# Attention's tables computed on the chip in place of five loads, and the second chunk's q loaded and scored earlier

## The chip, the cores and the metric

The kernel runs on one core of a Trainium2 chip. The metric is the device time of one execution in microseconds (us). Before the change it is 579.93 us, the median of three runs (579.83 to 580.10).

## What is computed

A decaying linear attention is followed by two feed-forward layers. Cut to what matters (q, k and v are 2 x 8 x 768 x 64, the layers have 1536 tokens of 512 features):

```python
gamma = 1.0 - 2.0 ** (-5.0 - np.arange(H))
for t in range(S):
    state = gamma * state + outer(k[:, :, t], v[:, :, t])
    y[:, :, t] = (q[:, :, t] @ state) / np.sqrt(D)
x = y.transpose(0, 2, 1, 3).reshape(B * S, H * D)
xn = x / np.sqrt(np.mean(x * x, -1) + 1e-6) * rms_g
x = (silu(xn @ w_gate) * (xn @ w_val)) @ w_out
h = x @ w_in
out = np.maximum(0.01 * h, h) @ moe2_w_out
```

## The kernel before

**Attention by chunks.** The 1536 tokens are cut into 12 chunks of 128, six for each batch entry. A chunk needs two loads of 512 KB: `qkT` (q and k by feature, called q0 to q11 in the list of loads) and `kv` (k and v by token, k0 to k11). On TensorE a chunk c is scored (`sc`, line 187), its keys, scaled by their decay (`kd`, lines 160 and 168), are multiplied with v to the state's increment (`ou`, line 213), the running state is applied to the decayed q (`yi`, line 238) and the masked scores to v (`he`, line 254). VectorE multiplies the scores with the mask (`ds`, line 199), makes the decayed keys of six chunks (`kd`, line 160; ScalarE makes those of four, line 168), updates the state (`up`, lines 228 and 230) and adds up squares (`fa`, `sa`, lines 281 and 286). GpSimd multiplies q by its decay (`qs`, line 176). ScalarE squares the output and applies the gains (`sq`, `xg`, lines 266 and 274). `qs` of a chunk c has to stand ahead of its `yi`, `ds` ahead of `he`, `kd` ahead of `ou`, and `ou` ahead of `up`.

**Tables.** The mask (128 x 2 x 4 x 128 float32), the decay of q (`qdec_sb`), of the keys (`kdecs`), of the state (`sdecs`), the gains `rms_g` and an identity come from the host. `kdecs` and `sdecs` are loaded for the first of their places only; the others are powers of it: a matmul (`across`, line 1186) spreads the state's decays over the partitions, a reciprocal (line 1195) makes `turn` of them, and four multiplications (line 1197) and three (line 1206) fill the tables.

**What sets the order.** All loads but one stand in SyncE's queue in the order of the string `LOADS` (line 39): q and k as above, m the mask (two transfers), g the gains, s and d the decays of state and q, i the identity, w a weight tile (line 396). `kdecs` is loaded from ScalarE's queue (line 1177). The instructions of every engine up to the middle of the first layer's first group are written out by hand in `ORDER` (lines 48 to 62), one token for a step: `sc0` scores chunk 0, `wm1` runs four matmuls on zeros into the bank that the scores of chunk 1 will take, `tb`, `ts` and `tk` make the tables, `load` queues the loads of q11 and k11, g0:P to g0:L convert a weight tile. Each engine keeps the order of the tokens. Before the first token, seven matmuls on zeros (`keep_warm`, line 189) run on TensorE.

**After attention.** The steps behind `ORDER` are placed by a planner that gives costs to conversions and evacuations; TensorE then runs weight products without a break to the end.

Of the kernel before, what the change touches and what calls it, by code (L numbers as in the profile page):

```python
# [8 lines left out]
F32 = mybir.dt.float32  # L9
# [4 lines left out]
AF = mybir.ActivationFunctionType  # L14
ALU = mybir.AluOpType
AX = mybir.AxisListType

P = 128
CH = 128
# [16 lines left out]
SEVEN1 = (1, 2)  # L36
RAWS = 3
WARM = 7
LOADS = "q0 k0 m g s k1 q1 d q2 q3 k2 k3 q4 k4 q5 w w q6 w q7 k6 k8 k7 k5 i q8 q9 k9 q10 k10"
EARLY = 5  # L40
FIXED = 14
PLAIN = ("g0", "g1", "v0", "v1")
# [3 lines left out]

KD = (0, 1, 2, 3, 6, 7)
ORDER = """
sc0 kd0 ou0 ds0 tb ts wm1 tk he0 load kd1 up0 sc1 sq0 qs1 xg0 ou1 ds1 qs2 sc2 up1 fa0 yi1 qs3 ds2 he1 kd2 sa0 ou2 kd3
sq1 sc3 xg1 fa1 up2 qs4 yi2 ds3 kd4 ou3 sa1 sc4 up3 qs5 sc5 ds4 g0:P yi3 ds5 ou4 g1:P g0:1 he2 up4 g0:2 he3 g1:1 sq2  # L50
g0:3 to0 xg2 fa2 g1:2 sc6 me0 sa2 sq3 g0:4 sc7 xg3 ds6 rs0 v0:P yi4 kd6 ds7 ou6 qs7 kd8 he4 up6 yi5 kd7 v0:1 sq4 fa3
ou7 g0:H fa4 he5 sa3 xg4 g0:L up7 sq5 v0:2 sc8 sa4 xg5 fa5 v0:3 sc9 qs9 ds8 yi7 kd9 ds9 qs8 ou8 sp0 v0:4 to1 up8 qs10
# [13 lines left out]
def chain_kernel(ctx: ExitStack, tc: tile.TileContext, qk_t, kv, w1, w2, mask, qdec, kdec, sdec, rms_g, ident, out):  # L66
    nc = tc.nc
    NCHUNK = kv.shape[0]
    NPAIR = 4
    D = 64  # L70
# [3 lines left out]
    CPB = NCHUNK // 2  # L74
# [16 lines left out]
    const = attn_pools.enter_context(tc.tile_pool(name="const", bufs=1))  # L91
# [4 lines left out]
    mask_sb = const.tile([P, 2, NPAIR, CH], F32, name="mask_sb")  # L96
    qdec_sb = const.tile([P, NPAIR, CH], F32, name="qdec_sb")
    kdecs = const.tile([P, CPB - 1, 2 * NPAIR, 1], F32, name="kdecs")
    sdecs = const.tile([P, CPB - 2, NPAIR, 1], F32, name="sdecs")
    turn = const.tile([P, 2, NPAIR], F32, name="turn")  # L100
    g_sb = const.tile([P, NPAIR, 1], F32, name="g_sb")
    ident_sb = const.tile([P, P], F32, name="ident_sb")
    ones = const.tile([P, 1], F32, name="ones")
    expo = const.tile([P, 2], F32, name="expo")
    one_of = const.tile([P, 2], F32, name="one_of")
    ready = const.tile([P, 2], F32, name="ready")
    state = [const.tile([P, NPAIR, D], F32, name=f"state{i}") for i in range(4)]

# [3 lines left out]
    def acc_bank(i, name):  # L112
        return ps_acc.tile([P, 512], F32, tag=f"acc{i}", name=name)
# [7 lines left out]

    ch = {}
    xh, xl, xg = {}, {}, {}
    tables = {"d": (qdec_sb, qdec), "s": (sdecs[:, 0], sdec), "g": (g_sb, rms_g), "i": (ident_sb, ident)}

    def load(*items):
        for what in items:
            n, c = what[0], int(what[1:] or 0)
            if n == "w":
                fetch()  # L130
            elif n == "m":
                for j in range(2):
                    nc.sync.dma_start(out=mask_sb[:, j], in_=mask[:, j])
            elif n in tables:
                nc.sync.dma_start(out=tables[n][0], in_=tables[n][1])
            else:
                if c not in ch and EARLY <= c < EARLY + len(SPARE):
                    t = xp.tile([P, 4, 512], F32, tag=SPARE[c - EARLY], name=f"qkv{c}")
                    ch[c] = {"qkT": t[:, :2], "kv": t[:, 2:]}
                elif c not in ch:  # L140
                    ch[c] = {m: units.tile([P, 2, 512], F32, tag="u", name=f"{m}{c}") for m in ("qkT", "kv")}
                if n == "q":
                    nc.sync.dma_start(out=ch[c]["qkT"], in_=qk_t[c])
                else:
                    nc.sync.dma_start(out=ch[c]["kv"], in_=kv[c])

    nrm = {}

    def block_of(c):
        return max(i for i in range(NB) if offs[i] <= c * CH)  # L150
# [38 lines left out]
    def keep_warm(c, n=WARM):  # L189
        s = ch.setdefault(c, {})  # L190
        s["sc"] = ps_sc.tile([P, 2, NPAIR, CH], F32, tag="sc", name=f"sc{c}")
        for _ in range(n):
            nc.tensor.matmul(out=s["sc"][:, 0], lhsT=warm[:, :P], rhs=warm, start=True, stop=True)
# [197 lines left out]
    def fetch():  # L391
        if fetched[0] < min(len(sources), taken[0] + RAWS):
            key, src = sources[fetched[0]]
            fetched[0] += 1
            raw[key] = raws.tile([P, 512, 2], I32, tag="raw", name=f"raw_{key}")
            nc.sync.dma_start(out=raw[key].rearrange("p n two -> p (n two)"), in_=src.bitcast(I32))
# [108 lines left out]
    def queue(unit):  # L505
        key, after, ops = unit
        cost = COST_SUM if dict(wq)[key] is None else COST
        take = lambda names: [(key, *cost[n], ops.pop(n)) for n in names if n in ops]
        if key in index and dict(wq)[key] is None:
            converting.extend(tails + take("123H4h"))  # L510
            tails[:] = take("Ll")
            return
        converting.extend(take("P12"))
        if after is not None and ("P" in opened_units[after][2] if after in opened_units else True):
            converting.append((after, *COST["P"], lambda: prepare(after)))
        converting.extend(tails + take("34H"))
        tails[:] = take("L")
# [410 lines left out]
    def in_pairs(ops):  # L928
        both = [[ops[n] for n in (f"{i}", f"h{i}") if n in ops] for i in range(4)]
        return [lambda b=b: [do() for do in b] for b in both if b] + [ops[f"l{i}"] for i in range(4) if f"l{i}" in ops]  # L930
# [236 lines left out]
    steps = plan()  # L1167

    warm = const.tile([P, 512], mybir.dt.bfloat16, name="warm")
    nc.vector.memset(warm, 0.0)  # L1170
    nc.vector.memset(ones, 1.0)
    nc.vector.memset(expo, -0.5)
    nc.vector.memset(one_of, 0.0)
    for j in range(2):
        nc.vector.memset(one_of[j * D:j * D + 1, j:j + 1], 1.0)
    nc.scalar.activation(out=ready, in_=expo, func=AF.Silu)
    nc.scalar.dma_start(out=kdecs[:, 0], in_=kdec)
    load(*LOADS.split())

    def pair(p):  # L1180
        return 2 * p, 2 * p + 1

    def across():
        nrm["bank"] = acc_bank(3, "norm")
        for j in range(2):
            nc.tensor.matmul(
                out=nrm["bank"][:, j * NPAIR:(j + 1) * NPAIR],
                lhsT=one_of[:, j:j + 1].to_broadcast([P, P]),
                rhs=sdecs[:, 0, :, 0],
                start=True,  # L1190
                stop=True,
            )

    def tables_k():
        nc.vector.reciprocal(out=turn, in_=nrm["bank"][:, :2 * NPAIR].rearrange("p (j a) -> p j a", j=2))
        for i in range(1, CPB - 1):
            nc.vector.tensor_tensor(
                out=kdecs[:, i, :, 0].rearrange("p (a j) -> p j a", j=2),
                in0=kdecs[:, i - 1, :, 0].rearrange("p (a j) -> p j a", j=2),
                in1=turn,  # L1200
                op=ALU.mult,
            )

    def tables_s():
        for i in range(1, CPB - 2):
            nc.vector.tensor_tensor(out=sdecs[:, i], in0=sdecs[:, i - 1], in1=sdecs[:, 0], op=ALU.mult)

    terms = {}

# [11 lines left out]
    def layers():  # L1221
# [6 lines left out]
    }  # L1228
    by_pair_of = {"to": total, "me": mean, "rs": rsqrt, "sp": spread, "xs": scaled, "hi": high, "lo": rest}
    alone = {  # L1230
        "open": reopen, "layers": layers, "load": lambda: load("q11", "k11"), "tk": tables_k, "ts": tables_s,
        "tb": across,
    }
    by_step = {"M": product_high, "N": product_low, "C": consume}

    def do(token):
        if token in alone:
            alone[token]()
        elif ":" in token:
            convert_step(*token.split(":"))  # L1240
        elif token[:2] in by_chunk:
            by_chunk[token[:2]](int(token[2:]))
        elif token[:2] in by_pair_of:
            by_pair_of[token[:2]](pair(int(token[2:])))
        elif token[0] == "T":
            terms.pop(token[1:])()
        else:
            n, f, b = token[1], int(token[2]), int(token[3])
            if token[0] in by_step:
                by_step[token[0]](n, f, b)  # L1250
            elif token[0] == "D":
                down(0, f, b)
            else:
                (upper if token[0] == "U" else lower)((n, f, b))

    with tc.manual_schedule():
        keep_warm(0)
        for token in ORDER.split():
            do(token)
        for unit in opened_units.values():  # L1260
            if unit[2]:
                queue(unit)
        sums.extend(in_pairs(terms))
# [98 lines left out]
```

## Time and profile before

| | before |
|---|---|
| median of three runs | 579.93 us |
| time of the profiled execution | 579.99 us |
| its span in the trace | 578.2 us |
| TensorE (PE) busy | 567.9 us (98%) |
| VectorE (DVE) busy | 498.5 us (86%) |
| ScalarE (ACT) busy | 404.6 us (70%) |
| GpSimd (POOL) busy | 39.3 us (7%), 48 instructions |
| share of 16 DMA engines of SyncE's and ScalarE's transfers | 27.2% |

The span is the time from the first to the last instruction of the program; 1.79 us of the execution's own time lie around it. PEld is the weight load of TensorE, SPq, POOLq and so on the sequencers that issue and wait. All times of rows are counted from the span's start. A row of instructions ends, in brackets, with the idle time of the engine before it and what ended it. A row with "x7" merges seven instructions, and its time is that from the first's start to the last's end; matmuls are pipelined, so a busy TensorE need not be one at its peak.

### The profile page before, as it was taken

Reading aid. Unit: us, or ns where it says so; the run is one execution under the profiler, and the core shown is the slowest. Engines: PE = TensorE matmul, PEld = TensorE weight load, DVE = VectorE, ACT = ScalarE, POOL = GpSimd, SP = SyncE. Lnnn points to the kernel's source line nnn. Section 1 sums busy time; section 2 is a strip of 40 time slices with the busy share of each in tenths; the row PEclk is TensorE's granted clock in tenths of the full one; section 3 lists DMA queues with packets and bytes.
Section 4 is the critical chain, followed back from the end, with each engine's and each line's share of the span. In section 5 each row is a group of like instructions: output and inputs, shape, how many; then the busy total and the mean of one; then the engine's idle time right before and its main releaser. Section 6 shows DMA issues by size and latency. Waiting matters only on the chain.

```text
span 578.2 us, 8479 instructions
## 1 busy us (share of the span) xinstructions
PE 567.9 (98%) x3086; PEld 466.8 (81%) x3086; DVE 498.5 (86%) x920; ACT 404.6 (70%) x738; POOL 39.3 (7%) x48
## 2 busy tenths in 40 slices
PE   8899999999999999999999999999999999999997
PEld 5788788888888888888888878878888888888886
DVE  5799989986676899977899999999999989995793
ACT  2789767986666557877647589989867985676330
POOL 2332100010000000001000100000100020002100
PEclk9999999999999999999999999999999999999999
DMA  8991332442101221326220222224412253101545
GB/s 333 409 394 56 110 109 74 140 149 77 54 26 68 74 74 37 109 73 146 73 74 0 74 73 74 73 74 135 157 54 88 78 121 99 37 1 23 124 85 135
DMA packets 34922, 60.13 MB, mean 104 GB/s; under 512 B 19392, under 2 KB 19776, under 8 KB 34880
## 3 DMA queue, kind: packets, MB, share of 16 engines
q1 hardware_dynamic: 31728, 52.24, 27.2%
q0 software_dynamic: 3008, 7.34, 5.6%
q8 instruction: 24, 0.39, 0.3%
q14 instruction: 18, 0.15, 0.1%
q10 hardware_dynamic: 144, 0.00, 0.0%
HBM read 51.19 MB, written 8.39 MB: 103 GB/s over the span
## 4 chain that ended last, share of the span: by engine, by line
PE 87%; DMA 6%; DVE 4%; ACT 2%; issue 1%; SPq 0%; POOL 0%; DVEq 0%; POOLq 0%; ACTq 0%
PE X L795 11%; PE ao L625 9%; PE Z L795 8%; PE iX L995 8%; PE i L594 8%; PE ap L625 7%; PE v L594 7%; PE g L594 6%; PE vX L995 5%; PE gX L995 5%; PE iZ L995 4%; PE vZ L995 2%; PE gZ L995 2%; DMA qkv<-in_qk_t 2%; PE iY L995 2%; DMA qkv<-in_kv 2%
## 5 line engine op out<-in xcount | busy, mean ns | idle before, releaser
L625 PE MATMUL ap<-w_p,gp_0h 128*128 128x512 f32 (+1 forms) x130 | 39.7, 386 | 0.0
L594 PE MATMUL i<-x2h,w_i 128*128 128x512 f32 x128 | 32.3, 389 | 0.0
L594 PE MATMUL g<-xh,w_g 128*128 128x512 f32 x128 | 31.8, 390 | 0.0
L594 PE MATMUL v<-xh,w_v 128*128 128x512 f32 x128 | 31.7, 390 | 0.0
L625 PE MATMUL ao<-go_0h,w_o 128*128 128x512 f32 x96 | 31.0, 389 | 0.0
L625 PEld LDWEIGHTS ap<-w_p,gp_0h 128*128 128x128 f32 x130 | 24.3, 188 | 5.0
L594 PEld LDWEIGHTS g<-xh,w_g 128*128 128x128 f32 x128 | 23.9, 188 | 5.2 <-issue 0.2
L594 PEld LDWEIGHTS i<-x2h,w_i 128*128 128x128 f32 x128 | 24.0, 188 | 5.0
L594 PEld LDWEIGHTS v<-xh,w_v 128*128 128x128 f32 x128 | 23.9, 188 | 5.0
L625 PE MATMUL ap<-w_p,gp_0l 128*128 128x512 f32 (+1 forms) x65 | 25.1, 386 | 0.0
L933 ACT ACTIVATE more<-i 128x512 f32<-128x512 f32 x16 | 9.6, 599 | 22.1 <-PE i L594 22.0
L995 PE MATMUL iX<-th,w_si 128*128 128x512 f32 x64 | 20.7, 397 | 1.2 <-ACT iu L1012 0.7
L625 PEld LDWEIGHTS ao<-go_0h,w_o 128*128 128x128 f32 x96 | 18.0, 188 | 3.7
L995 PE MATMUL iZ<-x2h,w_si 128*128 128x512 f32 x64 | 20.2, 391 | 0.0
L497 DVE TENSOR_TENSOR w_o<-wa_o,w_o 128x512 fp32r<-128x512 f32 x12 | 8.2, 686 | 12.1 <-ACT w_o L493 12.1
L625 PE MATMUL ao<-go_0l,w_o 128*128 128x512 f32 x48 | 18.7, 389 | 0.0
L594 PE MATMUL g<-xl,w_g 128*128 128x512 f32 x64 | 17.2, 391 | 0.0
L594 PE MATMUL v<-xl,w_v 128*128 128x512 f32 x64 | 17.2, 391 | 0.0
L199 DVE TENSOR_TENSOR a<-sc,mask_sb 128x1024 f32<-128x1024 f32 (+1 forms) x13 | 14.5, 1135 | 3.1 <-PE sc L187 3.0
L826 DVE TENSOR_TENSOR y2acc<-X,y2acc 128x512 f32<-128x512 f32 x26 | 17.0, 681 | 0.2 <-PE X L795 0.2
L594 PE MATMUL i<-x2l,w_i 128*128 128x512 f32 x64 | 17.1, 389 | 0.0
L995 PEld LDWEIGHTS iX<-th,w_si 128*128 128x128 f32 x64 | 11.8, 188 | 5.2 <-ACT iu L1012 1.4
(364 smaller groups left out, 1814.5 us busy)
## 6 DMA issues: line engine op xcount, KB each, us to landing
raw_i<-in_w SPq DMA_DIRECT2D x16, 512.0 KB, 3.6
raw_p<-in_w SPq DMA_DIRECT2D x16, 512.0 KB, 3.6
raw_g<-in_w SPq DMA_DIRECT2D x12, 512.0 KB, 3.6
raw_v<-in_w SPq DMA_DIRECT2D x12, 512.0 KB, 3.4
raw_o<-in_w SPq DMA_DIRECT2D x12, 512.0 KB, 3.5
qkT<-in_qk_t SPq DMA_DIRECT2D x7, 512.0 KB, 6.6
kv<-in_kv SPq DMA_DIRECT2D x7, 512.0 KB, 8.1
out<-more POOLq DMA_DIRECT2D x12, 256.0 KB, 5.1
```

What stands on the lines that cost most here:

```text
L199: nc.vector.tensor_tensor(out=s["a"][:, j], in0=s["sc"][:, j], in1=mask_sb[:, j], op=ALU.mult)
L497: v.tensor_tensor(out=u[:, 1, :], in0=a, in1=u[:, 0, :].bitcast(F32), op=ALU.subtract)
L594: nc.tensor.matmul(out=dst, lhsT=lhs, rhs=rhs, start=(n == 0), stop=(n == len(pairs) - 1), skip_group_check=True)
L625: nc.tensor.matmul(out=acc["b"][m][:, c:c + cut], lhsT=lhs, rhs=rhs[:, c:c + cut], start=(start and n == 0), stop=(stop and n == 2), skip_ ...
L795: nc.tensor.matmul(out=acc[side][m], lhsT=lhs, rhs=rhs, start=(start and f == fs[0] and k == 0), stop=(f == fs[-2] and k == 2), skip_group ...
L826: nc.vector.tensor_tensor(out=dst, in0=banks[m], in1=dst, op=ALU.add)
L933: nc.scalar.activation(out=a, in_=x, func=AF.Prelu, alpha=0.01)
L995: nc.tensor.matmul(out=dst, lhsT=lhs, rhs=rhs, start=(start and n == 0), stop=(n == 5), skip_group_check=True)
```

## The change

The loads of the mask, of both decays (q and state) and of the identity are gone. The gains move to ScalarE's queue. GpSimd makes a ramp (`iota`, column minus partition) in the place of the identity and sets 56 single columns to constants. VectorE compares the ramp with zero (`tri`), fills the mask's tile with the powers of every head's decay by seven doublings, and scales it row by row with the decay of the keys and `tri`; ScalarE copies the powers into `qdec_sb` in between. This stands ahead of the first token. `kdecs` beyond its second place and `sdecs` are made later (`tk`), the identity by a comparison of the ramp (`id`). In the list of loads q1 and k1 come second, and in the order of the work `wm1` follows `sc0`, `sc1` and `qs1` come ahead of `he0`, `sc2` comes behind `yi1`.

```diff
-LOADS = "q0 k0 m g s k1 q1 d q2 q3 k2 k3 q4 k4 q5 w w q6 w q7 k6 k8 k7 k5 i q8 q9 k9 q10 k10"
+LOADS = "q0 k0 q1 k1 q2 q3 k2 k3 q4 k4 q5 w w q6 w q7 k6 k8 k7 k5 q8 q9 k9 q10 k10"
...
 ORDER = """
-sc0 kd0 ou0 ds0 tb ts wm1 tk he0 load kd1 up0 sc1 sq0 qs1 xg0 ou1 ds1 qs2 sc2 up1 fa0 yi1 qs3 ds2 he1 kd2 sa0 ou2 kd3
+sc0 wm1 kd0 ou0 ds0 sc1 qs1 he0 load kd1 up0 sq0 xg0 ou1 ds1 qs2 up1 fa0 yi1 sc2 qs3 ds2 tk id he1 kd2 sa0 ou2 kd3
 sq1 sc3 xg1 fa1 up2 qs4 yi2 ds3 kd4 ou3 sa1 sc4 up3 qs5 sc5 ds4 g0:P yi3 ds5 ou4 g1:P g0:1 he2 up4 g0:2 he3 g1:1 sq2
...
-    turn = const.tile([P, 2, NPAIR], F32, name="turn")
+    turn = const.tile([P, 2 * NPAIR], F32, name="turn")
...
-    one_of = const.tile([P, 2], F32, name="one_of")
+    steps_of = const.tile([P, 4, 2 * NPAIR, 1], F32, name="steps_of")
...
-            elif n == "m":
-                for j in range(2):
-                    nc.sync.dma_start(out=mask_sb[:, j], in_=mask[:, j])
-            elif n in tables:
-                nc.sync.dma_start(out=tables[n][0], in_=tables[n][1])
...
-    nrm = {}
+    nrm = {"bank": acc_bank(3, "norm")}
+    heads_of = [(j, a, 1.0 - 2.0 ** (-5.0 - 2 * a - j)) for j in range(2) for a in range(NPAIR)]
+    powers = mask_sb.rearrange("p j a t -> p (j a) t")
+    tri = state[3].rearrange("p a d -> p (a d)")[:, :CH]
+
+    def constants():
+        nc.gpsimd.iota(
+            ident_sb, pattern=[[1, CH]], base=0, channel_multiplier=-1, allow_small_or_imprecise_dtypes=True
+        )
+        for i, (j, a, g) in enumerate(heads_of):
+            nc.gpsimd.memset(powers[:, i, 0:1], g / D ** 0.5)
+        for k in range(4):
+            for i, (j, a, g) in enumerate(heads_of):
+                nc.gpsimd.memset(steps_of[:, k, i], g ** (8 << k))
+        for j, a, g in heads_of:
+            nc.gpsimd.memset(turn[:, 2 * a + j:2 * a + j + 1], g ** -CH)
+        for j, a, g in heads_of:
+            nc.gpsimd.memset(sdecs[j * D:(j + 1) * D, 0, a], g ** CH)
+
+    def decays():
+        nc.vector.tensor_scalar(tri, ident_sb, 0.0, None, ALU.is_ge)
+        for k in range(7):
+            n = 1 << k
+            out = powers[:, :, n:2 * n]
+            if k < 3:
+                nc.vector.scalar_tensor_tensor(
+                    out=out,
+                    in0=powers[:, :, :n],
+                    scalar=D ** 0.5,
+                    in1=powers[:, :, n - 1:n].to_broadcast([P, 2 * NPAIR, n]),
+                    op0=ALU.mult,
+                    op1=ALU.mult,
+                )
+            else:
+                nc.vector.tensor_tensor(
+                    out=out,
+                    in0=powers[:, :, :n],
+                    in1=steps_of[:, k - 3].to_broadcast([P, 2 * NPAIR, n]),
+                    op=ALU.mult,
+                )
+        for j in range(2):
+            own = slice(j * D, (j + 1) * D)
+            nc.scalar.activation(out=qdec_sb[own], in_=mask_sb[own, j], func=AF.Copy)
+        tables_k(1, 2)
+        for j, a, _ in heads_of:
+            nc.vector.scalar_tensor_tensor(
+                out=mask_sb[:, j, a],
+                in0=mask_sb[:, j, a],
+                scalar=kdecs[:, 1, 2 * a + j],
+                in1=tri,
+                op0=ALU.mult,
+                op1=ALU.mult,
+            )
+
+    def identity():
+        nc.vector.tensor_scalar(ident_sb, ident_sb, 0.0, None, ALU.is_equal)
...
     warm = const.tile([P, 512], mybir.dt.bfloat16, name="warm")
+    constants()
     nc.vector.memset(warm, 0.0)
     nc.vector.memset(ones, 1.0)
     nc.vector.memset(expo, -0.5)
-    nc.vector.memset(one_of, 0.0)
-    for j in range(2):
-        nc.vector.memset(one_of[j * D:j * D + 1, j:j + 1], 1.0)
-    nc.scalar.activation(out=ready, in_=expo, func=AF.Silu)
-    nc.scalar.dma_start(out=kdecs[:, 0], in_=kdec)
-    load(*LOADS.split())
...
-    def across():
-        nrm["bank"] = acc_bank(3, "norm")
-        for j in range(2):
-            nc.tensor.matmul(
-                out=nrm["bank"][:, j * NPAIR:(j + 1) * NPAIR],
-                lhsT=one_of[:, j:j + 1].to_broadcast([P, P]),
-                rhs=sdecs[:, 0, :, 0],
...
-    def tables_k():
-        nc.vector.reciprocal(out=turn, in_=nrm["bank"][:, :2 * NPAIR].rearrange("p (j a) -> p j a", j=2))
-        for i in range(1, CPB - 1):
...
-    def tables_s():
-        for i in range(1, CPB - 2):
-            nc.vector.tensor_tensor(out=sdecs[:, i], in0=sdecs[:, i - 1], in1=sdecs[:, 0], op=ALU.mult)
+    def tables_k(first=2, end=CPB - 1):
+        for i in range(first, end):
+            nc.vector.tensor_tensor(
+                out=kdecs[:, i, :, 0], in0=kdecs[:, i - 1, :, 0], in1=turn, op=ALU.mult
+            )
+            if i > 1:
+                nc.vector.tensor_tensor(out=sdecs[:, i - 1], in0=sdecs[:, i - 2], in1=sdecs[:, 0], op=ALU.mult)
...
+    nc.scalar.dma_start(out=kdecs[:, 0], in_=kdec)
+    nc.scalar.dma_start(out=g_sb, in_=rms_g)
+    nc.scalar.activation(out=ready, in_=expo, func=AF.Silu)
+    load(*LOADS.split())
+
     with tc.manual_schedule():
         keep_warm(0)
+        decays()
         for token in ORDER.split():
             do(token)
```

## Rows read from the trace of the kernel before

**Rows 1.** The page's chain that ended last, its shares of the span by engine.
```profile
PE 87%; DMA 6%; DVE 4%; ACT 2%; issue 1%; SPq 0%; POOL 0%; DVEq 0%; POOLq 0%; ACTq 0%
```

**Rows 2.** The chain of waits, first 110 us: start, time and what, in us.
```profile
2.12 4.96 DMA mask_sb<-in_mask
...
27.29 9.14 DMA qkv<-in_kv
...
69.38 3.87 PE g L594 x16
```

**Rows 3.** Stretches: busy us of PE, PEld, DVE, ACT, POOL; granted clock, DMA share, GB/s.
```profile
0.00:10.00 10.00, 7.91 (x63) 4.46 (x63) 4.42 (x19) 1.49 (x2) 0.20 (x4) 1.00 0.80 299
10.00:20.00 10.00, 9.50 (x162) 8.11 (x160) 7.74 (x14) 3.54 (x12) 5.19 (x4) 1.00 1.03 408
...
69.00:569.00 500.00, 498.71 (x2197) 410.20 (x2194) 437.70 (x800) 357.41 (x615) 19.92 (x28) 1.00 0.28 81
```

**Rows 4.** The loads that go, first 60 us: KB each, us from issue to landing.
```profile
mask_sb<-in_mask SPq DMA_DIRECT2D x2, 256.0 KB, 4.8
qdec_sb<-in_qdec SPq DMA_DIRECT2D x1, 256.0 KB, 5.4
ident_sb<-in_ident SPq DMA_DIRECT2D x1, 64.0 KB, 9.1
kdecs<-in_kdec ACTq DMA_DIRECT2D x1, 4.0 KB, 3.9
```

**Rows 5.** GpSimd's instructions in order of time, first 50 us: start, us.
```profile
0.24 0.10 POOL L1355 MEMSET const-float32-0.0<- 128x1 f32 x1 [0.24 <-issue]
...
0.34 0.10 POOL L1355 MEMSET const-uint8-127<- 128x1 uint8 x1
10.56 3.92 POOL L176 TENSOR_TENSOR qs<-qkT,qdec_sb 128x512 f32<-128x512 f32 x3 [10.11 <-DMA qdec_sb<-in_qdec]
```

**Rows 6.** Line 176 in the first 15 us: what GpSimd's sequencer does for it.
```profile
L176 POOLq MODIFY_POOL_CONFIG  x2: 8/10/11, 0.7 to 0.8; - x2
```

**Rows 7.** VectorE, with a load and an instruction of ScalarE, in order of time.
```profile
0.74 0.40 ACTq L1177 DMA_DIRECT2D kdecs<-in_kdec  x1
...
5.80 0.69 DVE L160 TENSOR_TENSOR kd<-kv,kdecs 128x512 f32<-128x512 f32 x1 [4.40 <-DMA kv<-in_kv]
...
8.45 0.78 DVE L1197 TENSOR_TENSOR kdecs<-kdecs,turn 128x8 f32<-128x8 f32 x4
...
10.12 0.60 ACT L266 ACTIVATE sq<-y 128x512 f32<-128x512 f32 x1 [7.45 <-PE y L254]
...
14.41 0.68 DVE L160 TENSOR_TENSOR kd<-kv,kdecs 128x512 f32<-128x512 f32 x1
15.00 0.28 DVE L286 TENSOR_TENSOR ss<-sq 128x128 f32<-128x128 f32 x1
...
16.96 1.23 DVE L199 TENSOR_TENSOR a<-sc,mask_sb 128x1024 f32<-128x1024 f32 x1
...
22.24 1.23 DVE L199 TENSOR_TENSOR a<-sc,mask_sb 128x1024 f32<-128x1024 f32 x1 [1.32 <-PE sc L187]
```

**Rows 8.** TensorE in order of time, first 45 us.
```profile
1.19 3.17 PE L193 MATMUL sc<-warm 128*128 128x512 bf16 x7 [1.19 <-DVE one_of L1173]
...
4.45 1.61 PE L187 MATMUL sc<-qkT 64*128 64x128 f32 x16
...
6.54 0.69 PE L213 MATMUL u<-kv,kd 128*64 128x64 f32 x16 [0.47 <-DVE kd L160]
...
10.00 1.16 PE L187 MATMUL sc<-qkT 64*128 64x128 f32 x16
...
12.95 1.09 PE L238 MATMUL y<-qs,state 64*64 64x128 f32 x16
```

**Rows 9.** VectorE's later waits for keys, 27 to 46 us.
```profile
28.58 0.94 DVE L160 TENSOR_TENSOR kd<-qkv,kdecs 128x512 f32<-128x512 f32 x1 [0.30 <-DMA qkv<-in_kv]
...
31.14 0.69 DVE L160 TENSOR_TENSOR kd<-qkv,kdecs 128x512 f32<-128x512 f32 x1 [0.15 <-DMA qkv<-in_kv]
```

More of the change, by code (lines that the diff above doesn't have):

```diff
@@ L123, in chain_kernel @@
     xh, xl, xg = {}, {}, {}
-    tables = {"d": (qdec_sb, qdec), "s": (sdecs[:, 0], sdec), "g": (g_sb, rms_g), "i": (ident_sb, ident)}
     def load(*items):
@@ L1172, in chain_kernel @@
     nc.vector.memset(expo, -0.5)
-    nc.vector.memset(one_of, 0.0)
-    for j in range(2):
-        nc.vector.memset(one_of[j * D:j * D + 1, j:j + 1], 1.0)
-    nc.scalar.activation(out=ready, in_=expo, func=AF.Silu)
-    nc.scalar.dma_start(out=kdecs[:, 0], in_=kdec)
-    load(*LOADS.split())
     def pair(p):
         return 2 * p, 2 * p + 1
-    def across():
-        nrm["bank"] = acc_bank(3, "norm")
-        for j in range(2):
-            nc.tensor.matmul(
-                out=nrm["bank"][:, j * NPAIR:(j + 1) * NPAIR],
-                lhsT=one_of[:, j:j + 1].to_broadcast([P, P]),
-                rhs=sdecs[:, 0, :, 0],
-                start=True,
-                stop=True,
-            )
-    def tables_k():
-        nc.vector.reciprocal(out=turn, in_=nrm["bank"][:, :2 * NPAIR].rearrange("p (j a) -> p j a", j=2))
-        for i in range(1, CPB - 1):
[L1197 to L1202, printed above, removed]
-    def tables_s():
-        for i in range(1, CPB - 2):
-            nc.vector.tensor_tensor(out=sdecs[:, i], in0=sdecs[:, i - 1], in1=sdecs[:, 0], op=ALU.mult)
+    def tables_k(first=2, end=CPB - 1):
+        for i in range(first, end):
+            nc.vector.tensor_tensor(
+                out=kdecs[:, i, :, 0], in0=kdecs[:, i - 1, :, 0], in1=turn, op=ALU.mult
+            )
+            if i > 1:
+                nc.vector.tensor_tensor(out=sdecs[:, i - 1], in0=sdecs[:, i - 2], in1=sdecs[:, 0], op=ALU.mult)
     terms = {}
@@ L1230, in chain_kernel @@
     alone = {
-        "open": reopen, "layers": layers, "load": lambda: load("q11", "k11"), "tk": tables_k, "ts": tables_s,
-        "tb": across,
+        "open": reopen, "layers": layers, "load": lambda: load("q11", "k11"), "tk": tables_k,
+        "id": identity,
     }
```

## The prediction

> **What bounds the kernel now.** I began with the shares of the chain that ended last [rows 1]: TensorE holds 87% of it, transfers 6%, VectorE 4%. The chain in order of time says where the rest lies [rows 2]: it runs through the mask's transfer, then through those of chunks until 27.29 + 9.14 = 36.43 us, crosses ScalarE and VectorE, and from 69.38 us is TensorE's alone. The table of stretches confirms it [rows 3]: from 69 to 569 us TensorE is busy 498.71 of 500 us, so whatever arrives late or early at 69 us moves the end by as much. Before that it is not the bound: in the first 10 us it is busy 7.91 with seven matmuls on zeros among them, and VectorE only 4.42. From 10 us on the DMA engines stand at a share of 1.03 and move 408 GB/s. So the change is decided ahead of 69 us, by two things: when the loads of chunks land, and when VectorE and TensorE can begin on chunk 0.
>
> **What goes.** The mask (2 x 256 KB), the decay of q (256 KB) and the identity (64 KB) are 0.85 MB [rows 4], and at 408 GB/s [rows 3] 2.1 us of a full queue. The loads behind them, from q2 on, land up to 2.1 us sooner; q1 moves ahead of k1 into the mask's place, so k1 lands where it did. With the tables go four small matmuls, a reciprocal and seven tiny VectorE instructions ahead of `he0`; all seven of the latter come back, one with the mask and six (`tk`) behind `ds2`, at 0.78/4 = 0.195 us each where each waits for the last [rows 7]; the six are two chains side by side, and I take 0.75 for them. This is the gain: 2.1 us at most, if nothing else is late.
>
> **What is added, up to the first decayed keys.** In the kernel before, `kd0` starts at 5.80 us, when k0 has landed [rows 7]. Behind the change VectorE has the whole making of the mask ahead of it, and call D the time at which `kd0` can start. Everything hangs on I, the start of the ramp on GpSimd, because VectorE's first added instruction compares the ramp, VectorE keeps its order, and the 56 columns stand behind the ramp in GpSimd's queue.
>
> I is what no row gives. Of GpSimd the trace shows four memsets at 0.24 to 0.34 us, and then nothing until the first `qs` at 10.56 [rows 5]. Between them its sequencer runs two MODIFY_POOL_CONFIG, of 8 and 11 ns, at 0.7 to 0.8 us, and they carry the line of that first `qs` [rows 6]: they belong to the first arithmetic on GpSimd, not to the memsets. Whatever they set going is not in their own 19 ns, and the wait for the decay of q, which ends at 10.56, would cover up to 9.7 us of it. The ramp would be the first arithmetic behind the pair, with no load to wait for. So I lies between 0.9 (the pair sets nothing going) and 10.56 (the first time at which such an instruction is seen to run). The row that is nearest in kind is the `qs` at 10.56 and not the memsets, which ran ahead of the pair; I take 8.0, on its side of the middle.
> The Trainium skill speaks against the change here: its page GPSIMD Engine Reference, section 2.1 Instruction dispatch, says that the first call behind a newly loaded library of GpSimd's pays some 6 us, with no instruction to be seen in the profile. By that rule, as an estimate, I would be 6.8 and the forecast 584.2 us.
>
> From I to D, in order:
> - The ramp, 128 columns, one stream: between a memset's 0.10 and a `qs` of four times the columns, 3.92/3 = 1.31 [rows 5]. I take a quarter of that, 0.33.
> - The comparison of 128 columns and its hop from GpSimd: VectorE's sum over 128 columns takes 0.28 [rows 7]; 0.3.
> - Seven doublings that each need the one before: three tiny ones at 0.195; 64 and 128 columns 0.2 each; 256 and 512 columns, scaled from the 0.69 of `kd0` [rows 7], 0.34 and 0.61. Together 1.95. They need 40 of the memsets by the last doubling; four memsets start within 0.34 - 0.24 = 0.10, some 0.034 apart [rows 5], and at 0.034 to 0.05 each (1.4 to 2.0 us) they keep ahead. At their whole 0.10 each (4.0) they would hold it back by about 2.2, and I keep that for the range.
> - ScalarE copies the powers out of the tile before VectorE may overwrite it: two copies, 0.60 each [rows 7], some 1.2 with the hop. The last four of the eight products into the mask follow the second copy, 4 x 0.21 (0.28 less what neighbours overlap) and a hop: 1.0. The other four, and the one step of `kdecs` (issued at 0.74 us [rows 7], landed 3.9 later [rows 4], at 4.6), hide under the copies.
> The sum is 0.33 + 0.3 + 1.95 + 1.2 + 1.0, about 4.8, so D = I + 4.8 = 12.8. For I = 0.9 it is `kdecs` that ends last: 4.7 + 0.2 + eight products at 0.21 + 0.1, D = 6.7.
>
> **From D to the scores of chunk 5.** I follow the new order by the durations of before [rows 7, 8]. `ou0` starts 0.74 behind `kd0` (5.80 to 6.54); TensorE then runs `ou0`, `sc1`, `he0`, `ou1`, `yi1`, `sc2` one behind the other, 0.69 + 1.16 + 1.09 + 0.69 + 1.09 + 1.16, less some 0.06 of overlap at each joint, so that `ds2` starts at D + 6.4; the masks and states of VectorE fit in between. `ds2`, `tk` and `id` are 1.15 + 0.75 + 0.1, so `kd2` starts at D + 8.4; from `kd2` to `ds3` it is 16.96 - 14.41 = 2.55 as before; from `ds3` TensorE's `yi2`, `ou3`, `sc4`, `sc5` take 3.95, and `ds5` starts at D + 14.9. In the kernel before it starts at 22.24, and waited 1.32 for q5. With D = 12.8 it is 27.7, 5.5 late; all loads it needs have then long landed.
> Behind it VectorE is nearly full until 69 us. What it can win back is its waits for keys, 0.30 and 0.15 [rows 9], since those land 2.1 us sooner: 5.5 - 0.45 = 5.05 late. `yi1` needs `qs1`, which follows the ramp, the memsets and ScalarE's copies (I + 3.8) and takes 1.31 [rows 5]: it is done by D + 0.4, and `yi1` starts at D + 4.25.
> **TensorE's clock.** It reads 1.00 in every stretch [rows 3]. With D = 12.8 TensorE has nothing to do from some 7.1 us (`sc0` and `wm1`) to 13.5, longer than any pause in the rows. If the grant falls, its first groups behind the pause take longer. The nearest row is `sc0`, the first real group: 1.61 against 1.16 of a later one [rows 8], 39% more. So it costs between nothing and 39% on all six groups, 2.2; I add one such difference, 0.45.
>
> Sum: 5.05 + 0.45 = 5.5 over the profiled execution's own 579.99 us (span 578.2 and 1.79 around it), 585.5; the median of the runs is 0.06 lower, so **585.4 us**.
>
> **The rivals.** *The ramp runs at once, and the change wins.* The place is GpSimd's queue at 0.9 us. For it: the memsets run 0.1 us each from the start [rows 5], and the pair itself is 19 ns [rows 6]. Against it: it needs the pair to have set nothing going. Then D = 6.7, `ds5` starts at 21.6, 0.64 sooner, and with the two waits for keys 1.1 us are won: 578.8. It can hardly be the whole 2.1, since `kd0` is later than before and VectorE, not the queue of loads, sets the pace from there. It decides as long as I is below 1.9, where I + 4.8 passes 6.7; from D = 7.8, at I = 3.0, the win is gone.
> *A short wait, and no difference.* With I between 1.9 and 4.2, or with I at 0.9 and memsets of 0.10 (the last doubling then waits until 5.2, D is 8), the earlier loads and the later start cancel: 579.9, within 1.2 us.
> *GpSimd ready only at 10.5 us, or a slow clock.* I = 10.4 adds 2.4 (587.8), and a slow first stretch of TensorE, or memsets of 0.10, some 2 more: up to 590.
> *The transfer is hidden anyway*: against this, the chain runs through it [rows 2].
>
> **How the numbers follow.** A measurement of this kernel can tell about 0.2% (1.2 us) from no change. A late ramp (I above 4.2) has 0.72: the pair's line and the empty 9.7 us fit it, and nothing in the trace excludes it. The ramp at once has 0.17, the short wait 0.11. The win of 1.1 us lies on the edge of what can be told, and I count 0.13 of the 0.17 beyond it (D may come at 6.2 as well). So faster 0.13, same 0.15, slower 0.72. The likeliest case by itself spans 582.5 to 588.5 (I from 5 to 10.5, the clock with or without). The range reaches over the win as well, from 578.5 to 588.4, and leaves out the sum of the worst bounds and a win of more than 1.4 us.
>
> **What would show it.** In the changed kernel's timeline: the iota's start (8 us, against 0.9); the seven doublings 1.95 us long; `kd0` at 12.8; TensorE idle ahead of `ou0`; `ds5` at 27.7 against 22.24; the solid TensorE stretch beginning near 75 us instead of 69.4; loads from q2 on landing about 2 us sooner. I am wrong if the iota starts within 2 us, and then `kd0` near 6.7 and a solid stretch near 68.3 us are to be seen; wrong in size if the chain from `kd0` to `ds5` isn't 14.9.

## The result, and the profile after it

The changed kernel takes **585.62 us** (median of 6 runs), the kernel before beside it 579.91: a ratio of 1.0089, 95% interval 1.0067 to 1.0111. It is slower by 5.7 us (some 5.2 by the ratio), close to the 585.4 forecast, but for another reason than the forecast's likeliest case. One run of 2036 us was disturbed: the median counts it (585.49 without it), the ratio does not. The profiled execution took 584.56 us with a span of 582.8; before it is 579.99 and 578.2.

The chain that ended last, and the stretches of [rows 1] and [rows 3] for the changed kernel (busy us of PE, PEld, DVE, ACT, POOL; granted clock, DMA share, GB/s), with one stretch more:

```profile
PE 89%; DVE 7%; ACT 2%; issue 1%; POOL 0%; DVEq 0%; POOLq 0%; ACTq 0%
```
```profile
0.00:10.00 10.00, 6.86 (x51) 3.65 (x52) 8.01 (x24) 2.75 (x4) 4.68 (x63) 1.00 0.80 308
10.00:20.00 10.00, 7.44 (x128) 6.43 (x126) 8.16 (x20) 5.50 (x19) 4.31 (x4) 0.96 1.03 409
20.00:30.00 10.00, 10.00 (x166) 9.25 (x167) 7.81 (x16) 4.95 (x13) 2.18 (x2) 0.86 1.03 408
69.00:569.00 500.00, 498.43 (x2199) 409.77 (x2198) 440.37 (x805) 360.30 (x620) 20.93 (x29) 1.00 0.28 80
```

The loads have left the chain (DMA held 6% of it), VectorE has taken their place (7% against 4%). In 10 to 20 us TensorE is busy 7.44 us instead of 9.50, and in 10 to 30 us its granted clock is no longer 1.00. The loads of chunks from q2 on landed 1.7 to 3.2 us sooner, where up to 2.1 was forecast (q5 at 18.57 us against 20.90). Still TensorE's solid stretch begins later, at 73.03 instead of 69.38 us [rows 2], and its last matmul is 3.74 us later; the chain in order of time:

```profile
71.32 1.01 POOL nr L355
...
73.03 3.89 PE g L643 x16
```

GpSimd's first instructions, in order of time (start, us; in brackets the idle time before and what ended it), which answer to [rows 5]:

```profile
0.83 0.24 POOL L147 IOTA ident_sb<- 128x128 f32 x1 [0.40 <-POOLq L1388]
1.02 0.32 POOL L151 MEMSET mask_sb<- 128x1 f32 x8
1.28 1.11 POOL L154 MEMSET steps_of<- 128x1 f32 x32
...
7.66 5.39 POOL L225 TENSOR_TENSOR qs<-qkT,qdec_sb 128x512 f32<-128x512 f32 x3 [4.64 <-DMA qkT<-in_qk_t]
15.34 1.27 POOL L225 TENSOR_TENSOR qs<-qkT,qdec_sb 128x512 f32<-128x512 f32 x1 [2.29 <-DMA qkT<-in_qk_t]
...
30.37 1.27 POOL L225 TENSOR_TENSOR qs<-qkv,qdec_sb 128x512 f32<-128x512 f32 x1
32.83 1.27 POOL L225 TENSOR_TENSOR qs<-qkv,qdec_sb 128x512 f32<-128x512 f32 x1 [1.18 <-DMA qkv<-in_qk_t]
34.98 1.47 POOL L225 TENSOR_TENSOR qs<-qkv,qdec_sb 128x512 f32<-128x512 f32 x1 [0.88 <-POOL qs L225]
```

The ramp starts at 0.83 us. The wait on which the forecast rested (8.0) does not exist. VectorE in order of time, which answers to [rows 7, 9]:

```profile
1.10 1.77 DVE L161 TENSOR_SCALAR state<-ident_sb 128x128 f32<-128x128 f32 x1
...
8.20 0.69 DVE L209 TENSOR_TENSOR kd<-kv,kdecs 128x512 f32<-128x512 f32 x1
...
15.51 1.12 DVE L1229 TENSOR_TENSOR kdecs<-kdecs,turn 128x8 f32<-128x8 f32 x1
...
16.66 0.17 DVE L1229 TENSOR_TENSOR kdecs<-kdecs,turn 128x8 f32<-128x8 f32 x1
...
17.02 0.22 DVE L196 TENSOR_SCALAR ident_sb<-ident_sb 128x128 f32<-128x128 f32 x1
17.16 0.69 DVE L209 TENSOR_TENSOR kd<-kv,kdecs 128x512 f32<-128x512 f32 x1
...
30.87 1.33 DVE L209 TENSOR_TENSOR kd<-qkv,kdecs 128x512 f32<-128x512 f32 x1
...
33.59 1.07 DVE L209 TENSOR_TENSOR kd<-qkv,kdecs 128x512 f32<-128x512 f32 x1
...
34.91 1.83 DVE L330 TENSOR_TENSOR sq<-sq 128x256 f32<-128x256 f32 x2
```

Equal instructions take unequal times. The comparison of the ramp takes 1.77 us while GpSimd writes its columns; its twin for the identity (L196) takes 0.22. A step of `kdecs` takes 1.12 us where a product of GpSimd runs (15.34 to 16.61), the next one 0.17. `kd6` at 30.87, `kd7` at 33.59 and the second of the two sums at 34.91 (the pair takes 1.83; it took 0.75 in other runs) each meet such a product. It goes the other way as well: `qs1` starts at 7.66 while VectorE's last products into the mask run, and takes 2.37 us for 1.27, while `kd0` behind them (8.20) takes its usual 0.69.

TensorE over the same time, to be read against [rows 8]:

```profile
14.25 1.09 PE L303 MATMUL y<-a,kv 128*64 128x128 f32 x16
17.90 0.69 PE L262 MATMUL u<-kv,kd 128*64 128x64 f32 x16 [2.56 <-DVE kd L209]
18.51 1.39 PE L236 MATMUL sc<-qkT 64*128 64x128 f32 x16
19.84 1.97 PE L287 MATMUL y<-qs,state 64*64 64x128 f32 x16
21.74 1.11 PE L262 MATMUL u<-kv,kd 128*64 128x64 f32 x16
```

It waits 2.56 us for `kd2`, and then its clock is granted at the lower of its two levels (1.2 GHz of 2.4) from 19.30 to 22.71 us: three groups take 1.39, 1.97 and 1.11 us for 1.16, 1.09 and 0.69, together 1.53 more.

### The profile page after: what moved, and what is told of

It reads as the page before. It is cut to its first block, busy times and chain, and to the rows that moved or that the text cites. A ratio compares the mean times of both kernels' runs of the same rounds, so it can differ in the third digit from the quotient of the medians.

```text
span 582.8 us, 8542 instructions
## 1 busy us (share of the span) xinstructions
PE 568.0 (97%) x3082; PEld 467.4 (80%) x3082; DVE 506.1 (87%) x933; ACT 405.7 (70%) x740; POOL 44.7 (8%) x105
## 4 chain that ended last, share of the span: by engine, by line
PE 89%; DVE 7%; ACT 2%; issue 1%; POOL 0%; DVEq 0%; POOLq 0%; ACTq 0%
PE X L844 11%; PE ao L674 9%; PE Z L844 8%; PE iX L1044 8%; PE i L643 7%; PE ap L674 7%; PE v L643 7%; PE g L643 6%; PE vX L1044 5%; PE gX L1044 5%; PE iZ L1044 4%; PE vZ L1044 2%; PE gZ L1044 2%; PE iY L1044 2%; DVE a L248 1%; PE gY L1044 1%
## 5 line engine op out<-in xcount | busy, mean ns | idle before, releaser
L315 ACT ACTIVATE sq<-y 128x512 f32<-128x512 f32 x12 | 7.1, 601 | 13.3 <-PE y L303 13.2
```

The source lines that it names most:

```text
L315: nc.scalar.activation(out=s["sq"], in_=s["y"], func=AF.Square)
```

## The experiments

Theory 1 was: the table work delays `kd0`, the comparison is held by GpSimd's memsets, and the pause costs TensorE its clock. Four runs went to it. Each time below is a median, beside the kernel before on the same chip.

**The comparison moved last.**

```diff
-        nc.vector.tensor_scalar(tri, ident_sb, 0.0, None, ALU.is_ge)
         for k in range(7):
...
+        nc.vector.tensor_scalar(tri, ident_sb, 0.0, None, ALU.is_ge)
         for j in range(2):
```

> The changed kernel, with the one comparison of the ramp (tri) moved behind the seven doublings, when GpSimd's 56 memsets are over. Theory 1 (VectorE's comparison was held while GpSimd wrote its memsets): it takes about 0.2 us there instead of 1.77, the doublings end about 1.5 us sooner unless the steps' memsets hold them (then 0.5 to 1.5), kd0 starts near 7.1 instead of 8.20, and 0 to 1 us of the total (585.6) comes back. Rival (the comparison is slow by itself, as VectorE's first work or its first use of the ramp): it takes 1.5 us or more wherever it stands, kd0 stays at 8.2, and the time stays at 585.6. A first doubling that now takes over 1 us would say that whatever stands first beside the memsets is held.

Measured 583.39 us (before 579.99; ratio 1.0053, 1.0035 to 1.0070), 2.2 below the changed kernel, where 0 to 1 was expected. VectorE in order of time:

```profile
3.96 0.22 DVE L180 TENSOR_SCALAR state<-ident_sb 128x128 f32<-128x128 f32 x1
...
7.10 0.69 DVE L209 TENSOR_TENSOR kd<-kv,kdecs 128x512 f32<-128x512 f32 x1
...
30.99 0.75 DVE L330 TENSOR_TENSOR sq<-sq 128x256 f32<-128x256 f32 x2
...
33.47 1.35 DVE L330 TENSOR_TENSOR sq<-sq 128x256 f32<-128x256 f32 x1
34.74 1.76 DVE L530 SCALAR_TENSOR_TENSOR wa_v<-raw_v,wa_v 128x512 int32<-128x512 int32 x1
```

The comparison takes 0.22 where no memset runs: it was held, not slow, and `kd0` comes 1.10 us sooner. But VectorE, 1.09 us ahead of the kernel before at 33 us (`sa` at 33.13 against 34.22), is 0.91 behind at 36.42 (`ds8`, 35.51 before): two instructions were held 2.01 us by products that ran from 33.00 to 35.95. Theory 1 did not have that. The first hold of `tk` was gone (0.16 for its first step), the pause ahead of `ou2` was 1.59 us, and the clock stayed at 1.00 there; it fell from 44.45 to 47.86 us instead, at another pause.

**Nine matmuls on zeros in TensorE's pause.**

```diff
-... qs3 ds2 tk id he1 kd2 sa0 ou2 kd3
+... qs3 ds2 tk id he1 wm3 kd2 sa0 ou2 kd3
```

> The changed kernel, with nine matmuls on zeros in the place where TensorE had nothing to do from 15.34 to 17.90 us (between he1 and ou2). Theory 1 (the pause cost the clock, and the clock cost time): the granted clock stays at 1.00 in 19 to 23 us, sc3, yi2 and ou3 fall from 1.39, 1.97 and 1.11 to about 1.2, 1.1 and 0.7, ds4 and ds5 start about 1.3 us sooner, and 0.3 to 1.3 us of the 585.6 come back. Rival (TensorE waits there anyway, the slower groups are hidden behind VectorE): the clock is mended, ds5 stays within 0.3 us of 25.13, the time within 0.3 of 585.6. If the nine matmuls are longer than the pause, ou2 and kd3 come later by as much and the total is above 585.6.

Measured 585.58 (ratio 1.0084, 1.0054 to 1.0114). It decides nothing: `sc3`, `yi2` and `ou3` went at 1.16, 1.09 and 0.69, but in this execution one of the eight products into the mask took 1.35 us for 0.35 beside a product of GpSimd, the pause ahead of `ou0` grew to 3.45 us, and the clock fell there (0.66 in 10 to 15 us).

**The table steps put back behind `ds0`.**

```diff
-sc0 wm1 kd0 ou0 ds0 sc1 ... qs3 ds2 tk id he1 kd2
+sc0 wm1 kd0 ou0 ds0 tk sc1 ... qs3 ds2 id he1 kd2
```

> The changed kernel, with the later steps of the two tables (tk) put back right behind ds0, where GpSimd multiplies nothing yet, out of the way between ds2 and kd2. Theory 1 (its first step was held 0.95 us by a qs of GpSimd, and TensorE waited 2.56 us for kd2 behind it): every step takes 0.17 us, kd2 comes 1 to 2 us sooner than 17.16, TensorE's pause ahead of ou2 falls under 1.2 us, no stretch of a lower granted clock follows, and 1 to 2.5 us of 585.6 come back. Rival (the steps cost the same wherever they stand, since VectorE is full): kd1 to ds2 come as much later as kd2 comes sooner, and the time stays at 585.6. A third outcome: the steps run beside qs1 (7.66 us) and are held there.

Measured 586.26 (ratio 1.0101, 1.0069 to 1.0132): the third outcome, though the product was the third and not `qs1`. A step of `sdecs` took 1.24 us for 0.16 beside it, a product into the mask 1.35 beside `qs1`, and `kd2` came at 17.82. The hold was moved, not removed. TensorE's pause of 3.02 us ahead of `ou0` was followed by no lower clock here; one of 2.56 us from 44.36 us on was.

**The three loads taken out of the kernel before.**

```diff
-LOADS = "q0 k0 m g s k1 q1 d q2 ... k7 k5 i q8 q9 k9 q10 k10"
+LOADS = "q0 k0 g s k1 q1 q2 ... k7 k5 q8 q9 k9 q10 k10"
...
+    nc.gpsimd.memset(mask_sb, 0.01)
+    nc.gpsimd.memset(qdec_sb, 0.1)
+    nc.gpsimd.memset(ident_sb, 0.01)
```

> The kernel before, its order of work unchanged, without the loads of the mask, the decay of q and the identity: these three tiles are filled with constants by GpSimd, so the mask, q's decay and the transposition by the identity are left out of what is computed. All else runs as before. It shows what the loads alone are worth. Theory 1 (the loads are worth nearly what I took, and the change gives it back elsewhere): loads from q2 on land 2 us sooner, the waits for keys go, and the time is 1.0 to 2.0 us below 579.9. Rival (the transfers were hidden behind VectorE anyway): within 0.5 us of 579.9.

Measured 584.81 (ratio 1.0056, 1.0029 to 1.0084): neither. With the old order, none of the new arithmetic on VectorE and 2 us sooner loads its median lost nearly what the change loses. Its 12 runs fall apart: three took 579.76 to 580.58 at a mean granted clock of 0.999 to 1.000, nine 584.23 to 586.02 at 0.993 to 0.997. Which instructions met in the runs that were not profiled is not known. VectorE, then GpSimd, in the profiled one, one of the nine:

```profile
8.38 3.95 DVE L1200 TENSOR_TENSOR kdecs<-kdecs,turn 128x8 f32<-128x8 f32 x4
```
```profile
8.57 3.75 POOL L176 TENSOR_TENSOR qs<-qkT,qdec_sb 128x512 f32<-128x512 f32 x3 [6.27 <-DMA qkT<-in_qk_t]
```

The four steps that took 0.78 us in [rows 7] take 3.95: three of them stand each behind one of the three products, which in the kernel before waited for q's decay until 10.56 us [rows 5] and now start with q1. TensorE then waits 2.48 us, and its clock falls (0.68 in 15 to 20 us). **Theory 2** came from this run: VectorE is nearly full from 25 to 69 us, so every instruction of its that a GpSimd product holds adds some 1.05 us, and some pauses of TensorE add slow groups. The kernel before stands where next to nothing meets; sooner loads move the products.

**The gate.** One column written by VectorE keeps the products of chunks 9, 8 and 10 until `ds8`, which reads PSUM.

```diff
+    def gate_q(c):
+        ch[c]["qs"] = gp.tile([P, NPAIR, CH], F32, tag="gl", name=f"qs{c}")
+        nc.vector.memset(ch[c]["qs"][:, 0, 0:1], 0.0)
...
-... fa5 v0:3 sc9 qs9 ds8
+... fa5 v0:3 gq9 sc9 qs9 ds8
```

> The run with the comparison moved last, and one thing more: VectorE writes one column of the tile of chunk 9's product (gq9) just ahead of ds8, so that GpSimd's three products for chunks 9, 8 and 10 can't start before it, and run beside ds8 and ds9, which read PSUM, instead of beside VectorE's sums at 33.5 and 34.7 us. Theory 2 (what gives the gain back are VectorE's instructions with both inputs in SBUF, each held about 1.05 us by a GpSimd product that runs when it starts): fa5 takes 0.42 instead of 1.35 and the step of wa_v 0.69 instead of 1.76, VectorE at ds8 stands 1.1 us ahead of the kernel before instead of 0.9 behind, no stretch of a lower clock follows near 44 us, and the time is 578.5 to 580.5, against 583.4 without the gate. Rival (the lower clock comes whatever the products do, and it makes the loss): a stretch at the lower clock is still there, and the time stays above 582.

Measured **580.12** (before 580.27; ratio 0.9995, 0.9985 to 1.0004), 3.3 us less than without the gate (583.39, on another chip). VectorE, then GpSimd:

```profile
33.23 0.43 DVE L335 TENSOR_TENSOR sq<-sq 128x256 f32<-128x256 f32 x1
33.57 0.68 DVE L535 SCALAR_TENSOR_TENSOR wa_v<-raw_v,wa_v 128x512 int32<-128x512 int32 x1
34.18 1.22 DVE L253 TENSOR_TENSOR a<-sc,mask_sb 128x1024 f32<-128x1024 f32 x1
34.20 0.06 DVE L230 MEMSET qs<- 128x1 f32 x1
```
```profile
34.41 2.51 POOL L226 TENSOR_TENSOR qs<-qkv,qdec_sb 128x512 f32<-128x512 f32 x2 [6.54 <-DVE qs L230]
```

The two held instructions are back at 0.43 and 0.68, `ds8` beside the products at 1.22 is not held, and the clock reads 1.00 in every stretch up to 50 us: with VectorE in time, TensorE had no long pause there.

**The gate, and the table steps in VectorE's wait ahead of `ds2`.**

```diff
-... yi1 sc2 qs3 ds2 tk id he1 kd2
+... yi1 sc2 qs3 tk id ds2 he1 kd2
```

> The run with the gate, and tk and id moved ahead of ds2, into VectorE's wait of 0.73 us for sc2. Theory 2: kd2 comes 0.5 to 0.7 us sooner than 15.09, TensorE's pause ahead of ou2 falls from 1.6 to about 1 us, and 0.2 to 0.5 us more are won than by the gate alone, if VectorE's order and not TensorE sets the pace there; a total near 578. Rival (the products of GpSimd move with every change and meet other instructions): a new hold of about 1 us at another place, and the time is that of the gate alone or up to 2 us worse.

Measured 579.46 (ratio 0.9994, 0.9983 to 1.0005). `kd2` comes at 14.24, 0.60 sooner than with the gate alone, and the pause ahead of `ou2` is 0.90. The median is 0.66 us below that of the gate alone, but the two ratios (0.9994 and 0.9995) do not tell them apart, so the win is not shown. In the profiled execution TensorE's solid stretch begins at 67.76, 1.62 us ahead of the kernel before.

**The products left out**, of the changed kernel and, as a control, of the kernel before.

```diff
     def decay_q(c):
+        return
...
-                    rhs=s["qs"][r, a, :],
+                    rhs=qdec_sb[r, a, :],
```

> The changed kernel without GpSimd's products of q and its decay: yi multiplies the state by the table of the decay itself, so the product with q is left out of what is computed; all else runs as it did, the late comparison too. Theory 2: tk's first step takes 0.17, kd6 at most 0.9, kd7 0.69, fa5 0.42, which is 2.8 us less on VectorE behind 15 us, and the time is 582 to 583.5 against 585.6. Rival (the loss is the later kd0 and VectorE's added work, 2.4 us at kd0): within 0.7 us of 585.6. If it falls below 580, the products cost more than their holds.

> The control for the last run: the kernel before, with the same left out (the product of q and its decay; yi takes the table of the decay). Theory 2: there GpSimd's products hold VectorE by some 0.5 us in all (one sum at 12.69 and kd6), so the time is 579.9, at most 0.7 below. Rival (the products cost every version the same): 2 us or more below 579.9.

Measured 580.96 for the changed kernel (ratio 1.0008, 0.9999 to 1.0018) and 580.18 for the kernel before (1.0002, 0.9991 to 1.0012). The products cost the kernel before nothing and the changed one 4.7 us. VectorE in the changed kernel without them:

```profile
8.20 0.68 DVE L209 TENSOR_TENSOR kd<-kv,kdecs 128x512 f32<-128x512 f32 x1
...
15.50 0.16 DVE L1226 TENSOR_TENSOR kdecs<-kdecs,turn 128x8 f32<-128x8 f32 x1
...
16.18 0.68 DVE L209 TENSOR_TENSOR kd<-kv,kdecs 128x512 f32<-128x512 f32 x1
...
28.36 0.68 DVE L209 TENSOR_TENSOR kd<-qkv,kdecs 128x512 f32<-128x512 f32 x1
...
30.42 0.68 DVE L209 TENSOR_TENSOR kd<-qkv,kdecs 128x512 f32<-128x512 f32 x1
...
31.36 0.75 DVE L327 TENSOR_TENSOR sq<-sq 128x256 f32<-128x256 f32 x2
```

Up to `ds1` it runs as the changed kernel does, with `kd0` at 8.20. From there the rows of the two give each part: `tk` 0.98 (`kd2` at 17.16 against 16.18), the slow clock 1.53 (`ds5` stands at 25.13 against 22.62, that is 2.51 with `tk`), `kd6` 0.66, `kd7` 0.38, `fa` 1.08 (1.83 against 0.75): 4.63 in all. My 582 to 583.5 had counted the holds and not the clock.

**The loads' worth, with no product to meet.** The kernel before, without the three loads and without the products (both edits above).

> The kernel before without the three loads (mask, decay of q, identity filled with constants by GpSimd, so those are left out of what is computed) and without GpSimd's products (yi takes the constant table; the product of q and its decay is left out too). Theory 2: with no product to meet, the loads are worth what their bytes say: VectorE and TensorE stand 1.3 to 2.0 us ahead of the kernel before at 73 us, no instruction of VectorE is held, the end is 0.8 us longer, and the time is 578.6 to 579.5, against 584.8 with the products. Rival (the loads were hidden anyway): less than 0.5 us ahead at 73 us, and a time of 580 to 580.7.

Measured 578.89 (before 580.05; ratio 0.9981, 0.9971 to 0.9992). TensorE's solid stretch begins here:

```profile
67.02 3.85 PE g L591 x16
```

That is 2.36 us ahead of 69.38: at this place the loads are worth what their bytes say (2.1 us at 408 GB/s), and a little more. In the time it is 1.16 us: the way from the last matmul to the end is 0.62 longer (4.40 us against 3.78), and the profiled execution, 578.27, was the fastest of the nine. The same kernel with its products took 584.81, 5.9 us more.

**The clock by itself.** The run with the comparison moved last had a pause of 2.56 us at 41.6 us; nine matmuls on zeros were put ahead of it.

```diff
-... sq7 ou9 fa6 xg6 sc11 rs1
+... sq7 ou9 wm11 fa6 xg6 sc11 rs1
```

> The run with the comparison moved last, and nine matmuls on zeros between ou9 and sc11, ahead of the pause of 2.56 us in which TensorE waited for yi8 (41.6 to 44.2 us); VectorE's work and its holds stay as they are. It takes the lower clock by itself. Theory 2, its second part (the pause costs the clock, and the clock costs time): the clock stays at 1.00 in 44 to 48 us, the two groups yi8 and yi9 take 1.09 instead of 1.77 and 1.93, and the total falls from 583.4 by 0.5 to 1.5 us. Rival (VectorE's holds set the end, TensorE's slower groups are covered): the groups are faster, and the time stays within 0.3 us of 583.4.

Measured 581.77 (ratio 1.0035, 1.0023 to 1.0047), 1.62 less than 583.39. TensorE without the fill, then with it:

```profile
44.20 3.47 PE L287 MATMUL y<-qs,state 64*64 64x128 f32 x32 [2.56 <-issue]
47.60 0.79 PE L262 MATMUL u<-kv,kd 128*64 128x64 f32 x16
```
```profile
42.42 2.12 PE L242 MATMUL sc<-warm 128*128 128x512 bf16 x9
44.47 1.16 PE L236 MATMUL sc<-qkT 64*128 64x128 f32 x16
46.02 2.08 PE L287 MATMUL y<-qs,state 64*64 64x128 f32 x32 [0.39 <-POOL nr L355]
48.02 0.69 PE L262 MATMUL u<-kv,kd 128*64 128x64 f32 x16
```

The two groups of `yi` take 2.08 us instead of 3.47; the clock is 1.00 where it was 0.71 (45 to 50 us). The profiled execution with the fill reached `ou9` 1.94 us later than the one without (41.80 against 39.86; other holds ahead of it) and the group behind these three only 0.32 later (48.54 against 48.22). So 1.62 came back between these two places, as in the medians: the lower clock costs time of its own. The profiled execution, 583.59, is the slowest of the five; the other four took 581.64 to 581.81.

**The end of the kernel.** From the last matmul's end to the end of the span the kernel before takes 3.78 us, the changed one 4.63 (577.87 + 0.28 to 582.8), and every kernel with fewer issues on SyncE 4.40 to 4.66. The list of DMA issues of the changed kernel shows the last stores with more time from issue to landing (KB each, us):

```profile
out<-partial SPq DMA_DIRECT2D x3, 256.0 KB, 2.4
out<-partial SPq DMA_DIRECT2D x2, 128.0 KB, 2.3
```

They took 2.1 and 1.9 before. In the kernels with fewer issues on SyncE (129 here for 135), a fetch of 8 KB on the queue of instructions falls among these stores, here at 579.31 us; before it fell at 571.35, ahead of them.

```diff
-... q9 k9 q10 k10"
+... q9 k9 q10 k10 z0 z1 z2 z3 z4 z5"
...
+            elif n == "z":
+                nc.sync.dma_start(out=spare_row[:, c], in_=kdec[0:1])
```

> The run with the gate and the early steps, and six loads of 32 bytes more on SyncE's queue, behind the loads of chunks; nothing reads them. They bring SyncE's instructions back to as many as in the kernel before (135 issues instead of 129). In every kernel with fewer loads on that queue the way from the last matmul to the end took 4.56 to 4.64 us instead of 3.78, and a fetch of 8 KB on the instruction queue fell among the last stores instead of ahead of them. Theory 3 (what is lost at the end comes from where this fetch falls in SyncE's program): the fetch falls ahead of the last stores again, the end takes 3.78 us, and the time is 578.6, against 579.46 without the six. Rival (the end is longer for another reason, for instance where the tiles lie): it stays at 4.6 us and the time at 579.5. Should the six loads delay the loads of weights, VectorE's lead of 1.6 us at 73 us would be smaller.

Measured 579.37 (before 580.05; ratio 0.9990, 0.9981 to 0.9998). The fetch moved ahead of the stores (570.31), and the last wait for a store ended 2.91 us behind the last matmul, as before (3.47 in the changed kernel). So the longer stores go with the place of the fetch; how it holds them is not shown. The end still came after 4.20 us, 0.42 more than before, and SyncE's last ten waits show why. In the kernel before, those for the last three stores close the list. Here the last store's is the third, and the seven behind it take 0.06 us each, 0.42 in all (in the changed kernel the last three stores' are the third to fifth, and five follow, 0.30). The total hardly moved against 579.46. Of the versions that leave nothing out this is the only one whose interval lies below the kernel before, by 0.1%, less than can be told apart safely.

## Why the prediction came out right, and where it was wrong

- **The ramp's start, I = 8.0: wrong, and the forecast's main step.** It starts at 0.83. By my own sign ("I am wrong if the iota starts within 2 us") the likeliest case, given 0.72, did not come; nor did the win of the rival that had the ramp at once, given 0.17. The first `qs` at 10.56 [rows 5] was late for its load alone (it runs at 7.66 in the changed kernel, once q1 has landed), and the MODIFY_POOL_CONFIG pair [rows 6], which carries the ramp's line here, ends 0.05 us ahead of the ramp and set nothing going that can be seen.
  The rule of the Trainium skill's page GPSIMD Engine Reference, section 2.1 Instruction dispatch (some 6 us at a first call), does not show here; no run tells whether a library was newly loaded.
- **From I to D, 4.8: wrong in size.** From 0.83 to `kd0` at 8.20 it is 7.4. The comparison was held (1.77 for 0.3; without the hold `kd0` comes 1.10 sooner). The doublings ended 2.5 us behind it, for 1.95. The step that four of the eight products into the mask "hide under the copies" failed: all eight stood behind ScalarE's first copy and only its second ran beside them, 6.09 to 8.20, 0.26 each for 0.21; from the last doubling to `kd0` that is 2.8 for 2.2. By my own rivals D = 8.2 meant that nothing is won or lost ("from D = 7.8 the win is gone"), and that is what the changed kernel without the products measures (580.96 against 580.27).
- **From D to `ds5`, 14.9: right as a chain, wrong in this kernel.** It took 16.93. Without the products it is 22.62 - 8.20 = 14.42; the rest is 0.98 of `tk` held by a product, where I had taken 0.75 for all six steps, and 1.53 of clock.
- **Behind `ds5`, 0.45 won: wrong.** The lateness grew from 2.89 to 3.65, since three instructions met products (2.12 in all, of which 1.36 was won back). The prediction put this at nothing without a reason: no term and no rival had it that the products move with the loads and hold a full VectorE.
- **The clock, 0.45: the mechanism right, the size 1.53, and another pause** (ahead of `ou2`, not `ou0`). The row that sized it, `sc0` at 1.61, ran at a granted clock of 1.00 [rows 3] and was no sign of it; `yi2`, wholly in the slow stretch, took 1.97 for 1.09, 81% more and not 39%.
- **The end: not foreseen**, 0.85.
- **The loads, 2.1 us at most: nearly right** (2.36 at TensorE's solid stretch). The profiled execution's 4.57 us is then: without products 0.93 ahead at 73 us, products and their clock 4.63 the other way, the end 0.85.

So 5.5 forecast and 4.6 to 5.7 measured agree by chance.

## What to carry to other kernels

Before an input is made to land sooner, ask which instruction it releases and what that one will meet: here GpSimd's products start with a load and move with it, and a VectorE without slack paid for nearly every one that it met. Compare the time of equal instructions within a profile: where a 0.17 takes 1.12, look at what its neighbour ran meanwhile. Where they can't be kept apart by order, one column written by VectorE lets GpSimd's work start beside an instruction that reads PSUM (580.12 us against 583.39).

## What the runs showed of the hardware

- A VectorE instruction with both inputs in SBUF that starts while a GpSimd product has begun its work waits for that product's end: 0.17 became 1.12 to 1.27, 0.42 became 1.35 to 1.50. `ds` with its scores in PSUM took 1.22 beside a product. A product that starts while such instructions of VectorE run waits for them (`qs1`: 2.37 for 1.27).
  This is the lock that the Trainium skill's page SBUF — State Buffer, section Who interferes with whom, describes, and the traces agree.
- A comparison with one input was held by memsets alone (1.77 against 0.22), so for it GpSimd need not read; with the comparison moved last, the first doubling, which has two inputs in SBUF, ran among the same memsets in 0.18. Beside a product an instruction with one input was held as well (the limiting of `wa_v` in the run without the three loads: 1.50 for 0.41). Some 50 memsets, 0.034 us apart, went by before the comparison ended.
- In the runs of this case seven pauses of TensorE lasted 2.44 to 3.45 us; at five of them the granted clock went to its lower level (1.2 GHz), at two (3.02 and 2.44 us) it stayed at 1.00. It stayed there at all of 1.94 us and less.
